# Fillers between the first-stage pieces taken out, a piece's folding moved to VectorE, and three pieces of work placed elsewhere in the start of a fused FFT and MLP kernel

## The chip, the cores and the metric

The kernel runs on one core of one Trainium2 chip. Its engines are TensorE (PE, matmuls into PSUM, with weight loads shown apart as PEld), VectorE (DVE), ScalarE (ACT), GpSimd (POOL) and SyncE (SP, which here only issues DMAs). The metric is device time in microseconds. The profile numbers time from the start of the profiled span.

## The reference

```python
x: (8, 3008, 256) float32         # 8 batches, 3008 = 47 * 64 rows, 256 columns
w_in: (256, 2048), w_out: (2048, 256)   # float64 as they arrive

X = fft(fft(x, axis=1), axis=2).real.astype(float32)
x = X.reshape(24064, 256)
h = x @ w_in
g = h * clip(h + 3, 0, 6) / 6
out = (g @ w_out).astype(float32)
```

A two-dimensional Fourier transform of each batch, of which the real part goes through an MLP with a hard-swish between its two products.

## The kernel before

**The transform.** The 3008 rows are taken as 47 x 64. Stage 1 is a transform of length 47 over the slow index, a matmul with the tables F; stage 2 joins the twiddles and the transform of length 64, a matmul with the tables T. The transform along the 256 columns is multiplied into `w_in` ahead of time by `fold_w_in` (C times a piece of `w_in` gives columns of W1, and one row of them goes by small DMAs into WN). Symmetry of a real input halves the work: rows n and 64 - n, and columns d and 256 - d, are added or subtracted first. That is the "fold". `fold_half(hb, m, part, eng)` does it for one piece of a single batch: part 0 adds the partner rows (fetched reversed in row order by a gather on GpSimd's DMA queue), part 1 adds and subtracts the mirrored columns into a new tile y. For batch 0, all pieces but one skip part 1's sums and differences: there TensorE does them, by reading the tile forward and backward and accumulating both in PSUM.

**The pieces.** The batches are worked in pairs. In the first pair, batch 0 and batch 1 are separate halves (`halves[0]`, `halves[1]`), each of four pieces in the order m = 3, 0, 1, 2 (`ORDER`). `stage1_early` takes one piece of batch 0: a few tiny matmuls into pt (column 128), then the piece's own into two PSUM banks (`ps1`, lines 320 to 330), then copies to an SBUF tile z (lines 336 to 338; the last of the last piece is VectorE's, the others ScalarE's), then DMAs of z to DRAM (zd). Only the rows that the first two groups need go at once (line 347); the rest is put into the list `later`, of which four transfers are issued at the end of step 1 and four at the end of step 3. A piece's PSUM banks come from a pool of four, its pt tiles from one of three. Tile z takes a buffer from a different pool for each piece: twice zpool, then ypool, then cpool.

**Groups.** `load_g_half` brings a group back from DRAM (line 414), `stage2_half` (line 433) makes q of it with a copy by ScalarE (line 436), `spread_half` and `spread_by_pe` copy its last row to all partitions (qn). Four groups per half feed eight chunks of 256 columns.

**The weights.** They arrive as float64, in 16 pieces of 128 x 512 numbers (`PIECES`; two of `w_in`, two of `w_out`, and again). Each piece j is loaded through GpSimd's DMA queue (`load_w`, lines 713 and 717) and turned to float32 in five parts: `exponent_a` (ScalarE, line 733, two activations into PM), `exponent_b` (TensorE, line 745, two matmuls into ex or spare), `exponent_c` (ScalarE, line 748), `mantissa` (VectorE, lines 756 and 757, into top), and `join` (VectorE, lines 765 or 771, into wi or G). `head_b(j)` is the mantissa and then, for j = 4 to 9, the load of piece j + 6. `mix_w_out` (GpSimd, lines 780 to 783) forms the combined blocks of G that later chunks need.

**Steps.** There are 384 steps, one for each chunk and each of eight parts of the hidden width. A step's MLP is `mlp1` (TensorE: products u and v, line 523, from a pool of three banks), `activate` (VectorE: s from u, WN and qn, line 532, then u and v, lines 542 and 544; ScalarE: t, line 569; VectorE: the gate, a, line 572), `combine` (GpSimd: c, line 586), and `mlp2` (TensorE, line 616, seven products for eight). Steps 0 to 7 are the first chunk, while the weights are still being prepared: there `mlp2_first` (line 596) uses eight plain products and needs no combine, and `first_steps` (even steps) and `second_steps` (odd) write out by hand how the weights' parts and the MLP's follow each other. Other work is put in at the start of a step by `beside` (`put(t, ...)`: step t): loads of T, groups, the folding and stage 1 of batch 1.

**What sets the order.** Nothing is reordered: each engine runs its instructions in the order in which the code issues them, and semaphores hold one until its data and its buffer are there. So a place in the code is a place in every queue that the call uses. `keep_awake(n)` (line 814) is n matmuls of 128 x 512 whose result nobody reads, called fillers here; the profile names them "awake" and shows two records for each. In the start they stand between the pieces (line 894), after them, and between the exponents' matmuls (lines 902 and 907). `see` (line 863) is a GpSimd copy that holds GpSimd's queue until the first group is back from DRAM; the loads of weight pieces 4 to 9 stand behind it.

Of the kernel before, what the change touches and what calls it, by code (L numbers as in the profile page):

```python
# [58 lines left out]
def kernel(  # L59
# [10 lines left out]
    nc = tc.nc  # L70
# [10 lines left out]
    XC = 4  # L81
    NS = N2 // 2
    NXC = NS // XC
    NM = NXC // 2
# [51 lines left out]


    ORDER = [NM - 1] + list(range(NM - 1))

    def x_tile(pool=xpool, tag="x"):  # L140
        return pool.tile([P, XC, D], F32, tag=tag, name="xt")
# [58 lines left out]
    def fold_half(hb, m, part, eng):  # L200
        xt, xr = hb.x[m][0:PX - 1], hb.xr[m][0:PX - 1]
        n = XC if m < NM - 1 else XC - 1
        a, r = xt[:, 0:n, :], xr[:, XC - 1:(XC - 1 - n) if n < XC else None:-1, :]
        lo, up = slice(0, N1), slice(PB, PB + N1)
        tt = eng.tensor_tensor
        if part == 0:
            sums = [(a, r)] + ([(xt[lo, n:XC, :], xr[lo, 0:1, :])] if n < XC else [])
            for a, r in sums:
                tt(a[:, :, 1:P], a[:, :, 1:P], r[:, :, D - 1:P:-1], op=AL.add)
                tt(a[:, :, D - 1:P:-1], a[:, :, D - 1:P:-1], r[:, :, 1:P], op=AL.add)  # L210
            return
        if hb.b == 0 and n == XC:
            tt(a[:, :, 0:P + 1:P], a[:, :, 0:P + 1:P], r[:, :, 0:P + 1:P], op=AL.add)
            return
        y = ypool.tile([PX - 1, XC + 1, D], F32, tag="y", name="y")
        hb.y[m] = y
        near, far = xt[:, :, 1:P], xt[:, :, D - 1:P:-1]
        tt(y[:, 0:XC, 1:P], near, far, op=AL.add)
        tt(y[:, 0:XC, P + 1:D], near, far, op=AL.subtract)
        tt(y[:, 0:n, 0:P + 1:P], a[:, :, 0:P + 1:P], r[:, :, 0:P + 1:P], op=AL.add)  # L220
        if n < XC:
            tt(y[lo, n, 0:P + 1:P], xt[lo, n, 0:P + 1:P], xr[lo, 0, 0:P + 1:P], op=AL.add)
            h = xr[up, 0, :]
            tt(y[up, XC, 1:P], h[:, 1:P], h[:, D - 1:P:-1], op=AL.add)
            tt(y[up, XC, P + 1:D], h[:, 1:P], h[:, D - 1:P:-1], op=AL.subtract)
            eng.tensor_copy(y[up, XC, 0:P + 1:P], h[:, 0:P + 1:P])
            eng.tensor_copy(y[up, n, 0:P + 1:P], xt[up, n, 0:P + 1:P])
        del hb.x[m], hb.xr[m]
# [74 lines left out]
    def stage1_early(hb, m):  # L303
        cosine, sine = slice(0, P + 1), slice(P + 1, D)
        last = m == NM - 1
        y = hb.y.pop(m) if last else hb.x[m]
        pt = [ps_h.tile([P, 2, 1], F32, tag="uv", name="pt") for h in range(2)]
        ps = [bank([P, 2, D], "ps1") for h in range(2)]
        quarters = [(i, h, 1 if last and h and i else 2) for i in range(2) for h in range(2)]
        for i, h, n in quarters:  # L310
            o = pt[h][i * PB:(i + 1) * PB]
            nc.tensor.matmul(o[:, 0:n], table(5, h), y[rows(h), 2 * i:2 * i + n, P:P + 1], start=True, stop=True,
                             skip_group_check=True)
            for k in range(2 if n < 2 else 0):
                nc.tensor.matmul(o[:, 1], table(k + 1, h), y[rows(h), XC - 1 + k, P:P + 1], start=(k == 0),
                                 stop=(k == 1), skip_group_check=True)
        if last:
            for i, h, n in quarters:
                o = ps[h][i * PB:(i + 1) * PB]
                nc.tensor.matmul(o[:, 0:n], table(0, h), y[rows(h), 2 * i:2 * i + n], start=True, stop=(n == 2),  # L320
                                 skip_group_check=True)
                for k, (j, cs) in enumerate([(XC - 1, cosine), (XC, cosine), (XC - 1, sine), (XC, sine)] if n < 2 else ()):
                    nc.tensor.matmul(o[:, 1, cs], table(k + 1, h), y[rows(h), j, cs], start=False, stop=(k % 2 == 1),
                                     skip_group_check=True)
        else:
            back = slice(D - 1, P, -1)
            for k, (t, to, fr) in enumerate([(0, cosine, cosine), (0, sine, slice(1, P)),
                                             (0, slice(1, P), back), (6, sine, back)]):
                for i, h, n in quarters:
                    nc.tensor.matmul(ps[h][i * PB:(i + 1) * PB, :, to], table(t, h), y[rows(h), 2 * i:2 * i + 2, fr],  # L330
                                     start=(k == 0), stop=(k > 1), skip_group_check=True)
        k = ORDER.index(m)
        pool, tag = ((zpool, "z"), (zpool, "z"), (ypool, "y"), (cpool, "c"))[k]
        z = pool.tile([PX, 2, 2, D + 1], F32, tag=tag, name="z")
        for h in range(2):
            nc.scalar.copy(z[:, h, :, D:], pt[h][0:PX])
        nc.scalar.copy(z[:, 0, :, 0:D], ps[0][0:PX])
        (nc.vector.tensor_copy if k == NM - 1 else nc.scalar.copy)(z[:, 1, :, 0:D], ps[1][0:PX])
        if not first.zd:
            first.zd[0] = dpool.tile([NG, 2 * KK, 2, NS, D + 1], F32, tag="zd0", name="zd")  # L340
        zd = first.zd[0][:].rearrange("g k c (h n) d -> (g k c) h (n d)", h=2)
        n0 = 2 * 4 * KK
        for i in range(2):
            n = (m * XC + 2 * i) * (D + 1)
            dst = zd[:, :, n:n + 2 * (D + 1)]
            src = z[i * PB:i * PB + PZ].rearrange("p h n d -> p h (n d)")
            (nc.scalar if k == NM - 1 and i else nc.sync).dma_start(out=dst[0:n0], in_=src[0:n0])
            later.append((dst[n0:], src[n0:]))
# [540 lines left out]
    for k, m in enumerate(ORDER):  # L889
        for part in range(2):  # L890
            fold_half(hb, m, part, nc.vector)
        stage1_early(hb, m)
        if k < NM - 1:
            keep_awake(1)
    load_g_half(hb, 0)

    seen = wpool.tile([P, 1], F32, tag="seen", name="seen")
    see(hb.g[0][:, 0, 0:1])
    for j in range(4, 10):
        load_w(j)  # L900

    keep_awake(2)
    for j in range(2, 4):
        exponent_a(j)
        mantissa(j)
        exponent_b(j)
        keep_awake(2)
    for j in range(2, 4):
        tail(j)

# [9 lines left out]
    def beside(p):  # L920
        ahead, behind = {}, {}

        def put(t, f, *a, at=ahead):
            at.setdefault(t, []).append((f, a))
# [3 lines left out]
        if p == 0:  # L928
            for gr in range(1, NG):
                put(gr + 1, load_t, gr)  # L930
            put(1, load_g_half, halves[0], 1)
            put(4, stage2_half, halves[0], 1)
            put(5, spread_half, halves[0], 1)
            put(NF - 1, close_w)
            for i, t in enumerate((3, 5, 7, 8)):
                put(t, mix_w_out, i)
            for gr in range(2, NSG):
                put(8 * gr - 10, load_g_half, halves[0], gr)
                put(8 * gr - 5, stage2_half, halves[0], gr)
                put(8 * gr - 4, spread_half, halves[0], gr)  # L940

            hb = halves[1]
            for k, m in enumerate(ORDER):
                put((1, 5, 8, 11)[k], take_half, hb, m, *((cpool, "c") if k == 0 else ()))
                put((1, 5, 8, 11)[k], load_half, hb, m, nc.sync)
                for part in range(2):
                    put((4, 6, 11, 14)[k] + part, fold_half, hb, m, part, nc.gpsimd)
                put((8, 10, 15, 18)[k], stage1_quarters, hb, m, at=behind)
            for gr in range(NSG):
                put(8 * gr + 23, load_g_half, hb, gr)  # L950
                put(8 * gr + 27 - (gr == 0), stage2_half, hb, gr)
                put(8 * gr + 28 - (gr == 0), spread_half, hb, gr)
# [75 lines left out]
    def second_steps(s):  # L1028
        j = 2 * s + 4
        if j - 2 < len(PIECES):  # L1030
            head_b(j)
            join(j)
            head_b(j + 1)
            if s == 1:
                mlp2_first(*chunk(s), halves=(0,))
                exponent_b(j + 1)
            exponent_c(j + 1)
            if j + 2 < len(PIECES):
                head(j + 2)
            join(j + 1)  # L1040
            if j + 3 < len(PIECES):
                head(j + 3)
            if s > 1:
                mlp2_first(*chunk(s), halves=(0,))
            mlp1(*chunk(s + 1))
            return
        mlp1(*chunk(s + 1))
        combine(*chunk(s + 1))
        mlp2_first(*chunk(s), halves=(0,))
        mlp1(*chunk(s + 2))  # L1050
        mlp2_first(*chunk(s), halves=(1,))
# [117 lines left out]
```

## Time and profile before

| | us |
|---|---|
| median of 3 runs (1943.94 to 1944.84) | 1944.27 |
| the profiled execution | 1943.62 |
| its span, from the first to the last instruction | 1941.9 |
| PE busy | 1924.4 (99%) |
| PE weight loads busy | 1659.3 (85%) |
| DVE busy | 1423.9 (73%) |
| ACT busy | 680.7 (35%) |
| POOL busy | 1435.6 (74%) |

In the lines below, a row of a timeline is: start, duration, engine, line, operation, output <- inputs, and in brackets how long the engine stood idle before it and what ended that. A row of the chain is: start, duration, what. "DMA share" is the mean busy share of the core's 16 DMA engines. A matmul in float32 shows as two records. Durations of matmuls hold the pipeline's end, so rows of one engine overlap a little. A wait for several semaphores is put down to the one that came last.

### The profile page before, as it was taken

What the parts mean: (1) busy time and instruction counts of PE and PEld (TensorE: products, weight loads), DVE (VectorE), ACT (ScalarE), POOL (GpSimd) and SP (SyncE); (2) the same over time, 40 slices, a digit from 0 to 9 for tenths busy, and PEclk for the clock granted to TensorE, in tenths of its full rate; (3) what the DMA queues carried; (4) which work ended last, traced back from release to release, by engine and by line L of the source; (5) the groups of instructions that cost most, each with busy time, mean ns of one, the idle gap of its engine ahead of it and who ended that gap; (6) DMA issues with size and microseconds to landing.
All of it is one profiled execution on the core that took longest, in us unless ns stands there. A gap on an engine that the chain in (4) does not pass through costs nothing.

```text
span 1941.9 us, 28190 instructions
## 1 busy us (share of the span) xinstructions
PE 1924.4 (99%) x9354; PEld 1659.3 (85%) x9354; DVE 1423.9 (73%) x2754; ACT 680.7 (35%) x1165; POOL 1435.6 (74%) x1644
## 2 busy tenths in 40 slices
PE   9999999999999999999999999999999999999998
PEld 5578888888988888888898888888899888888887
DVE  5876776677777777777787777777778777777777
ACT  5633333333333333333333333333333333333332
POOL 3397888887678877787678877878666667666665
PEclk9999999999999999999999999999999999999999
DMA  7532222311112222111111221222110101101000
GB/s 251 134 80 55 50 73 69 79 47 32 38 33 50 60 71 55 44 50 33 36 36 47 55 55 44 50 53 51 35 28 20 28 17 27 32 13 28 20 19 20
DMA packets 154520, 98.08 MB, mean 51 GB/s; under 512 B 121987, under 2 KB 136126, under 8 KB 154374
## 3 DMA queue, kind: packets, MB, share of 16 engines
q1 hardware_dynamic: 143106, 59.71, 12.8%
q0 software_dynamic: 10560, 36.35, 6.6%
q8 instruction: 73, 1.20, 0.3%
q14 instruction: 73, 0.60, 0.1%
q10 hardware_dynamic: 708, 0.23, 0.1%
HBM read 58.92 MB, written 37.32 MB: 50 GB/s over the span
## 4 chain that ended last, share of the span: by engine, by line
PE 93%; DVE 3%; ACT 1%; DMA 1%; POOL 1%; issue 1%; SPq 0%; DVEq 0%; ACTq 0%; POOLq 0%
PE acc L616 56%; PE v L523 16%; PE u L523 16%; PE ps L472 2%; PE ps L273 1%; DVE a L572 1%; DVE s L532 1%; PE awake L814 1%; ACT t L569 1%; DMA st<-in_moe_w_in_dram 0%; DVE o L677 0%; DVE u L553 0%; PE ps L433 0%; POOL c L586 0%; PE ps L330 0%
## 5 line engine op out<-in xcount | busy, mean ns | idle before, releaser
L586 POOL TENSOR_TENSOR c<-a 128x512 f32<-128x512 f32 (+1 forms) x375 | 468.1, 1248 | 355.5 <-PE acc L616 319.9
L616 PE MATMUL acc<-c,G 128*128 128x256 f32 (+1 forms) x3008 | 697.9, 375 | 0.9 <-POOL c L586 0.8
L569 ACT ACTIVATE t<-u,half 128x512 f32<-128x512 f32 (+1 forms) x384 | 260.6, 679 | 1145.4 <-DVE u L542 1066.0
L616 PEld LDWEIGHTS acc<-c,G 128*128 128x128 f32 x3008 | 566.6, 191 | 71.5 <-POOL c L586 2.1
L532 DVE SCALAR_TENSOR_TENSOR s<-qn,WN,u 128x256 f32<-128x256 f32 (+1 forms) x768 | 330.4, 472 | 345.5 <-PE u L523 340.0
L616 PE MATMUL acc<-a,G 128*128 128x256 f32 (+1 forms) x2256 | 542.1, 376 | 0.0
L616 PEld LDWEIGHTS acc<-a,G 128*128 128x128 f32 x2256 | 422.9, 190 | 71.9 <-issue 20.2
L523 PE MATMUL v<-q,W 127*128 127x256 f32 (+1 forms) x1536 | 389.6, 376 | 2.0 <-DVE a L572 2.0
L523 PE MATMUL u<-q,W 128*128 128x256 f32 (+1 forms) x1536 | 388.3, 376 | 0.2 <-ACT q L436 0.2
L572 DVE SCALAR_TENSOR_TENSOR a<-t,u 128x512 f32<-128x512 f32 (+2 forms) x448 | 264.0, 601 | 101.2 <-ACT t L569 97.6
L523 PEld LDWEIGHTS v<-q,W 127*128 127x128 f32 x1536 | 288.9, 190 | 42.0 <-DVE a L572 2.3
L523 PEld LDWEIGHTS u<-q,W 128*128 128x128 f32 x1536 | 286.6, 191 | 36.7 <-issue 2.4
L586 POOL TENSOR_TENSOR c<-c,a 128x256 f32<-128x256 f32 (+1 forms) x375 | 268.3, 715 | 29.4
L586 POOL TENSOR_TENSOR c<-a,c 128x256 f32<-128x256 f32 (+1 forms) x375 | 268.3, 715 | 29.4
L542 DVE TENSOR_TENSOR u<-s,v 128x512 f32<-128x512 f32 x352 | 245.1, 696 | 37.0 <-DVE s L532 0.5
L572 DVE SCALAR_TENSOR_TENSOR a<-t,v 128x512 f32<-128x512 f32 (+1 forms) x480 | 263.7, 566 | 0.1
L569 ACT ACTIVATE t<-v,half 128x512 f32<-128x512 f32 (+1 forms) x384 | 260.3, 678 | 0.2 <-PE acc L616 0.2
L544 DVE TENSOR_TENSOR v<-v,s 128x512 f32<-128x512 f32 x352 | 244.1, 693 | 0.0
L586 POOL TENSOR_TENSOR r<-w,e 128x256 f32<-128x256 f32 (+1 forms) x92 | 88.8, 986 | 3.6
L626 ACT ACTIVATE e<-acc 128x512 f32<-128x512 f32 (+2 forms) x184 | 83.3, 544 | 0.0
L677 DVE STREAM_TRANSPOSE o<-r 128x256 f32<-128x256 f32 (+1 forms) x192 | 72.5, 415 | 0.3
L586 POOL TENSOR_TENSOR w<-w,e 128x512 f32<-128x512 f32 (+1 forms) x46 | 57.5, 1249 | 3.6
(128 smaller groups left out, 776.6 us busy)
## 6 DMA issues: line engine op xcount, KB each, us to landing
out_dram<-o SPq DMA_DIRECT2D x747, 32.0 KB
g<-zd SPq DMA_DIRECT2D x42, 256.0 KB
zd<-z SPq DMA_DIRECT2D x48, 192.0 KB
xt<-in_x_dram POOLq DMA_DIRECT2D x22, 256.0 KB, 3.7
st<-in_moe_w_in_dram POOLq DMA_DIRECT2D x8, 512.0 KB, 6.4
st<-in_moe_w_out_dram POOLq DMA_DIRECT2D x8, 512.0 KB, 7.4
qn<-qd SPq DMA_DIRECT2D x16, 256.0 KB
xt<-in_x_dram POOLq DMA_DIRECT2D x17, 192.0 KB, 3.9
```

What stands on the lines that cost most here:

```text
L273: nc.tensor.matmul(ps[b][h * PB:(h + 1) * PB, 0:n], F[rows(b), 0:PB], y[rows(b), 2 * h:2 * h + n], start=True, stop=not last, skip_group_c ...
L472: nc.tensor.matmul(ps[:, blk, u * P:n].rearrange("p (b k) -> p b k", b=2), g[:, kk, blk * (P + 1):blk * (P + 1) + P], T[:, :, gr, blk, kk, ...
L523: nc.tensor.matmul(ps[:, i, 0:nq], W1[r, blk, f * P:(f + 1) * P], q[r, blk, of:of + nq], start=True, stop=True)
L532: nc.vector.scalar_tensor_tensor(s[:, i, 0:nq], qn[:, of:of + nq], WN[:, f:f + 1], u[:, i, 0:nq], op0=AL.mult, op1=AL.add)
L542: nc.vector.tensor_tensor(u[:], s[:], v[:], op=AL.add)
L544: nc.vector.tensor_tensor(v[:], v[:], s[:], op=AL.subtract)
L569: nc.scalar.activation(t, h, AF.Relu, bias=half[:], scale=scale)
L572: nc.vector.scalar_tensor_tensor(dst, t, 1.0, h, op0=AL.min, op1=AL.mult)
L586: (eng or nc.gpsimd).tensor_tensor(out, in0, in1, op=AL.add)
L616: nc.tensor.matmul(ch.acc[i // 2][:, i % 2, 0:ch.n], G[:, i, fc, :], mv, start=(fc == 0 and i % 2 == 0), stop=(fc == NF - 1), skip_group_c ...
L626: nc.scalar.mul(ch.e[:, k:i + 1, 0:ch.n], ch.acc[i // 2][:, 0:i + 1 - k, 0:ch.n], 1.0 / WS)
L677: nc.vector.transpose(o[:, 0:n // DH, h], ch.r[:, m, h, 0:n].rearrange("p (j i) -> p j i", i=DH))
```

## The change

- The three fillers between the first-stage pieces go, and one of the four after the weights' exponents that precede the second stage (`keep_awake(4 - j)`: two after piece 2, one after piece 3).
- The third piece of batch 0 (m = 1) is, like the first, folded wholly by VectorE, into a y tile; TensorE then does four matmuls of 512 columns for it. Its z comes from the activations' pool (apool) in place of ypool, and the list `later` is put in another order, so that this piece's remaining rows are written first.
- The second stage of batch 0's second group moves from the start of step 4 to step 3, ahead of the products of the next step.
- The first x of batch 1 is loaded through GpSimd's queue right behind weight pieces 4 to 9, in place of SyncE's queue at step 1.
- In step 1 the mantissa of piece 9, and with it the load of piece 15, comes after the MLP's first product and activation for step 2.

```diff
+    FULL = (ORDER[0], ORDER[2])
...
-        if hb.b == 0 and n == XC:
+        if hb.b == 0 and m not in FULL:
...
-        y = hb.y.pop(m) if last else hb.x[m]
+        y = hb.y.pop(m) if m in FULL else hb.x[m]
...
-        if last:
+        if m in FULL:
...
-        pool, tag = ((zpool, "z"), (zpool, "z"), (ypool, "y"), (cpool, "c"))[k]
+        pool, tag = ((zpool, "z"), (zpool, "z"), (apool, "a"), (cpool, "c"))[k]
...
         stage1_early(hb, m)
-        if k < NM - 1:
-            keep_awake(1)
+    later[:] = later[4:6] + later[0:4] + later[6:8]
     load_g_half(hb, 0)
...
     for j in range(4, 10):
         load_w(j)
+    take_half(halves[1], ORDER[0], cpool, "c")
+    load_half(halves[1], ORDER[0], nc.gpsimd)

     keep_awake(2)
     for j in range(2, 4):
         exponent_a(j)
         mantissa(j)
         exponent_b(j)
-        keep_awake(2)
+        keep_awake(4 - j)
...
             put(1, load_g_half, halves[0], 1)
-            put(4, stage2_half, halves[0], 1)
             put(5, spread_half, halves[0], 1)
...
             for k, m in enumerate(ORDER):
-                put((1, 5, 8, 11)[k], take_half, hb, m, *((cpool, "c") if k == 0 else ()))
-                put((1, 5, 8, 11)[k], load_half, hb, m, nc.sync)
+                if k > 0:
+                    put((5, 8, 11)[k - 1], take_half, hb, m)
+                    put((5, 8, 11)[k - 1], load_half, hb, m, nc.sync)
...
             if j + 3 < len(PIECES):
-                head(j + 3)
+                exponent_a(j + 3)
+                if s > 1:
+                    head_b(j + 3)
             if s > 1:
                 mlp2_first(*chunk(s), halves=(0,))
+            if s == 3:
+                stage2_half(halves[0], 1)
             mlp1(*chunk(s + 1))
+            if s == 1:
+                head_b(j + 3)
```

## The prediction

> **What bounds the kernel now.** I read the page's first part and its chain, then the busy time by stretch, then the chain in order of time over the first 120 us, and last each engine's timeline there. The stretches (columns: us; then PE, weight loads, VectorE, ScalarE, GpSimd busy with counts; granted clock; DMA share; GB/s):
>
> ```profile
> span 1941.9 us, 28190 instructions
> 0.00:36.00 36.00, 33.23 (x220) 17.48 (x220) 17.63 (x45) 20.78 (x34) 13.84 (x23) 1.00 0.70 218
> 36.00:60.00 24.00, 22.59 (x83) 14.21 (x82) 19.14 (x36) 16.33 (x28) 10.29 (x15) 1.00 0.80 256
> 60.00:80.00 20.00, 18.54 (x71) 11.95 (x70) 18.03 (x33) 13.42 (x22) 10.69 (x17) 1.00 0.57 159
> 105.00:120.00 15.00, 14.10 (x76) 10.39 (x75) 9.88 (x20) 4.73 (x9) 14.04 (x18) 1.00 0.28 70
> 120.00:400.00 280.00, 279.33 (x1343) 239.35 (x1342) 198.90 (x356) 99.71 (x173) 235.93 (x264) 1.00 0.27 65
> ```
>
> TensorE is busy nearly all the time, 279.33 of 280 us once the kernel is under way. Work that nothing touches follows the first 120 us, so whatever TensorE gains there reaches the end, unless a wait eats it. Within them it stands idle for 2.77, 1.41, 1.46 and, from 105, 0.90 us (each stretch less its busy time). But busy is not useful: the fillers ("awake") count as busy. The chain (start, us, what):
>
> ```profile
> 18.45 1.05 PE awake L814 x2
> ...
> 21.51 1.05 PE awake L814 x2
> ...
> 24.56 1.05 PE awake L814 x2
> ...
> 25.84 1.84 PE ps L330 x32
> 27.70 0.70 DVE z L338
> ...
> 33.21 1.72 PE awake L814 x4
> 34.93 0.91 PE ps L433 x8
> ```
>
> The four first-stage pieces run in a fixed rhythm, piece, filler, piece, filler, without a gap. After them come the weights' exponents with fillers, then the second stage at 34.93.
>
> **The change, part by part.**
>
> *Three fillers between pieces go.* 3 x 1.05 = 3.15 us of the chain, if the next piece is ready. VectorE's rows:
>
> ```profile
> 18.67 0.17 DVE L213 TENSOR_TENSOR xt<-xt 111x8 f32<-111x8 f32 x1
> 20.07 0.69 DVE L209 TENSOR_TENSOR xt<-xt 111x508 f32<-111x508 f32 x1 [1.23 <-DMA xt<-in_x_dram,IX]
> 21.27 0.17 DVE L213 TENSOR_TENSOR xt<-xt 111x8 f32<-111x8 f32 x1
> 22.04 0.59 ACT L338 COPY z<-ps 112x512 f32<-112x512 f32 x1
> ```
>
> The second piece can start at 18.45 and end near 20.5. The third fold was ready at 18.84, the fourth at 21.44, so folds do not hold it up.
>
> *Third piece folded fully.* TensorE gets 4 matmuls of 512 columns in place of 16 of 254 to 258. Nearest rows, both with the pipeline's end in them:
>
> ```profile
> 22.63 1.93 PE L330 MATMUL ps<-xt,F 47*64 47x258 f32 x32
> 105.61 1.08 PE L359 MATMUL ps<-y,F 47*64 47x512 f32 x8
> 14.56 0.68 DVE L219 TENSOR_TENSOR y<-xt 111x508 f32<-111x508 f32 x1
> ```
>
> -0.85 us on TensorE. VectorE gets two more 4 x 127 operations, some 0.6 us each from start to start: 1.2 us, which fit into the 1.23 us that it idled for the fourth piece's x. The fourth fold still ends near 21.45; without that pause it, and the fourth piece with it, would come up to 1.2 us later. The fourth piece waits for ScalarE to clear the second piece's banks: that piece ends near 20.5, two copies (0.59) and the small ones run to some 21.85, TensorE comes at 21.6. I charge 0.25. So the fourth piece ends 3.15 + 0.85 - 0.25 = 3.75 us sooner. If the fillers' time were wholly lost to waits, 0.85 would be left; without the 0.25 it is 4.0.
>
> *One filler less before the second stage* (2 of 4 records, half of 1.72): 0.86. Its cover is the group's arrival from DRAM, which GpSimd sees:
>
> ```profile
> 33.89 0.18 POOL L863 COPY seen<-g 128x1 f32<-128x1 f32 x1 [18.44 <-DMA g<-zd]
> 24.00:26.00 2.00, 2.00 (x30) 0.79 (x26) 0.00 (x0) 1.18 (x4) 0.00 (x0) 1.00 0.35 55
> ```
>
> 33.89 against 34.93: 1.04 us of slack. The write-out follows the fourth piece; the DMA share has fallen to 0.35 by 24 us, when it now starts, so I let the group come 3.75 sooner (30.14) and TensorE 3.75 + 0.86 = 4.6 (30.33). The next late thing is that group, 0.2 us behind. **Term A: 4.6, between 0.85 + 0.86 = 1.7 and 4.9.**
>
> *Mantissa of piece 9 behind step 2's activation.* The chain and timelines, in before's time:
>
> ```profile
> 56.70 0.49 DVE s L532
> 59.48 1.13 PE L523 MATMUL v<-q,W 127*128 127x256 f32 x4 [1.18 <-DVE a L572]
> 55.14 0.42 DVE L756 TENSOR_SCALAR top<-st 128x512 int32<-128x512 int32 x1
> 55.59 0.69 DVE L757 SCALAR_TENSOR_TENSOR top<-st,top 128x512 f32<-128x512 uint32 x1
> 64.89 1.07 DVE L756 TENSOR_SCALAR top<-st 128x512 int32<-128x512 int32 x1
> 65.99 1.23 DVE L757 SCALAR_TENSOR_TENSOR top<-st,top 128x512 f32<-128x512 uint32 x1
> 64.67 0.99 POOL L209 TENSOR_TENSOR xt<-xt 111x381 f32<-111x381 f32 x1 [3.95 <-DMA xt<-in_x_dram]
> ```
>
> VectorE's 1.06 us (55.14 to 56.20) come off ahead of step 2. But its second "s" is released by the WN transfer at 56.70, so the 1.18 us hole at 59.48 stays. **Term B: 0, at most 1.18**, if WN lands sooner. The 1.06 us come back between 60.1 and 61.2, ahead of step 3. There lies a trap: the same pair took 0.42 and 0.69 alone, 1.07 and 1.23 beside GpSimd's fold. If the moved pair met GpSimd, VectorE would be 1.2 us later still. Piece 15's load now waits for that mantissa, and behind the load on GpSimd's queue stand the mixing of the weights and the fold, so I expect no meeting there. GpSimd's 3.95 us of waiting for x, ahead of its fold at 64.67, hide this new wait of some 4.5 us all but 0.5: x is there long before, and the fold comes at about 65 as it did. The Trainium skill, "SBUF — State Buffer", section "Who interferes with whom", states that a VectorE operation with two SBUF inputs, or in a two-port mode, shares a port with GpSimd's reads; the two slow rows agree. By that rule, were the new x (already there) to let GpSimd fold just then, term C below would be near 0.
>
> *Second group's second stage ahead of step 4's products.*
>
> ```profile
> 72.31 0.88 DVE s L532 x2
> 74.72 0.69 DVE L572 SCALAR_TENSOR_TENSOR a<-t,u 128x512 f32<-128x512 f32 x1
> 68.97 2.76 ACT L733 ACTIVATE PM<-st,bias 128x512 uint8<-128x512 int16 x4
> 75.25 0.58 ACT L436 COPY q<-ps 128x512 f32<-128x512 f32 x1
> 75.88 0.59 PE L745 MATMUL ex<-PM,E 128*128 128x512 f16 x2 [1.46 <-ACT q L436]
> 77.77 0.86 PE v L523 x4
> ```
>
> The q copy stands on ScalarE behind step 4's relu; now it follows PM, ends by 72.3, and the 1.46 us hole at 75.88 goes. Next late is step 5's v: it takes the bank that step 4's gate (74.72, 0.69) frees, and VectorE is 1.06 late, so v starts at 76.5 instead of 77.77, and the products behind it (v takes 0.86) at 77.4 instead of 78.63. **Term C: 1.2, between 0 and 1.46.** The new u and v lie after the 0.9 us second stage, done by 72.5; VectorE wanted them at 72.31 and now near 73.4.
>
> *x of the second batch on GpSimd's queue.* Three issues (0.62 each, by SyncE's last of them) and the gather (1.00) come to 2.9 us and lie in GpSimd's 4.42 us of waiting:
>
> ```profile
> 43.12 0.72 POOL L717 DMA_DIRECT2D st<-in_moe_w_out_dram  x1 [4.42 <-DVE top L756]
> 45.21 1.00 POOL L172 DMA_INDIRECT xt<-in_x_dram,IX  x1 [0.30 <-issue]
> 56.24 0.62 SPq L197 DMA_DIRECT2D xt<-in_x_dram  x1
> ```
>
> Behind them on that queue stand the loads of pieces 10 and 11, the first to be late if 4.42 us do not do. Their bytes also queue behind 0.92 MB of x (twice 112 rows of 4 KB), 3.6 us at the 256 GB/s of 36 to 60. Both are covered by some 15 us, since the mantissa of piece 10 comes only at 64.89: 0. Without that cover it would cost TensorE those 3.6 us. SyncE loses three issues (the last at 56.24), so the group's second load and the leftover rows of z go out sooner; TensorE waits for neither now. The z of the third piece in the activations' pool: the leftovers written first are its own; 0. From 80 us on, VectorE, SyncE and GpSimd hang on TensorE's progress and move with it; the 0.90 us for GpSimd's products at 105 to 120 stays.
>
> **Sum.** 4.6 + 0 + 1.2 = 5.8 us. The profiled execution took 1943.62 us, 1.72 around its span; 1937.8. The median of the runs is 0.65 higher: 1938.5.
>
> **Rivals.** *Both holes close*: WN lands sooner and C is whole, A without its 0.25: 4.9 + 1.18 + 1.46 = 7.5, 1936.8. For it: SyncE and the DMA queues are freer. Against: WN's issues come before all that was removed.
>
> *Partly handed back*: the group from DRAM does not follow, or the moved mantissa meets GpSimd. With A = 3 and C = 0: 3.0, 1941.3. For it: only 0.2 us of slack left at 30.3. Against: the DMA share of 0.35 from 24 us.
>
> *The change does not bite*: the fillers only filled, and waits of the same length appear. A = 1.7, C = 0: 1942.6. Against: data for pieces 2, 3 and 4 are ready by the rows above.
>
> *Slower: the clock falls.* The fillers are named for keeping TensorE awake. At the kernel's end it idles from 1932.45, and the clock falls:
>
> ```profile
> 1930.99 1.46 PE L616 MATMUL acc<-c,G 128*128 128x192 f32 x8
> 1935.00:1942.00 7.00, 0.00 (x0) 0.00 (x0) 0.72 (x3) 0.00 (x0) 0.00 (x0) 0.66 0.25 55
> ```
>
> 0.66 over 7 us is 4.8 us at half: it fell some 4.8 us after the last matmul. If the quarter-array pieces, now on end from 16.6, did not count as work and the clock stood at half until the second stage, 13 us of work would double: 1944.27 - 5.8 + 13 = 1951.5. It loses from 5.8 us of work done at half rate, and shows as slower from 9.7. Against: the longest gap that I find in the new chain is some 0.5 us (the exponents' wait). The Trainium skill, "TensorE: Matmul & The Clock Gate", section "What's actually happening", puts the fall after an idle window of some 3.4 us; by that rule, as by the end's row, no gap here is long enough.
>
> **How the numbers follow.** Forecast (gain 4.6 to 6.6, 1937.6 to 1939.7) 0.52; both holes 0.16; partly handed back 0.18; does not bite 0.07; clock 0.07. About 0.2%, 3.9 us, is what a measurement of this kernel can tell. Faster: 0.52 + 0.16 + a third of the third, 0.74; same: the rest of it and the fourth, 0.19; slower 0.07. Range 1936.5 to 1942.3: both holes to most of the partly handed back, 0.84.
>
> **What would show it.** Right: pieces back to back from 18.4, the fourth ended near 24; the second stage near 30.3; no gap at the exponent after the q copy; the hole before v of step 3 still near 1.2, and a small one before v of step 5; clock 1.00. Wrong: a wait for g before the second stage over 0.5 us; VectorE's mantissa of piece 9 over 1.5 us; GpSimd's products waited for by more than 0.9 us at 100 to 115; a clock below 1.

## The result

The changed kernel takes 1940.45 us (median of 13 runs, 1938.39 to 1942.11) and the kernel before 1943.85 (13 runs beside them, 1942.70 to 1945.04): 3.4 us less, a ratio of 0.9981 with a 95% interval from 0.9972 to 0.9990. The direction and the range held; the size is some 60% of the 5.8 us forecast, and just short of the 0.2% that the text took as the bound of "faster". The profiled execution took 1940.75 us, 0.3 above the median. Its busy time by stretch (columns as in the prediction's first fence):

```profile
span 1939.0 us, 28126 instructions
0.00:36.00 36.00, 32.25 (x203) 18.65 (x204) 21.30 (x52) 22.01 (x37) 17.78 (x28) 1.00 0.76 247
36.00:60.00 24.00, 21.75 (x71) 12.73 (x70) 19.09 (x36) 16.48 (x27) 7.01 (x10) 0.94 0.95 279
60.00:80.00 20.00, 20.00 (x76) 12.74 (x75) 18.71 (x32) 13.66 (x23) 13.11 (x20) 0.99 0.30 79
```

From 60 to 80 the 1.46 us of idle time are gone, as forecast. From 36 to 60 there are 2.25 us of it where there were 1.41, the granted clock has fallen to 0.94, and the DMA share has risen from 0.80 to 0.95. That stretch was to stay as it was; here gain was given back. The chain of the start (start, us, what) carries no filler between pieces any more; the only fillers left in it stand among the weights' exponents:

```profile
20.04 0.29 PE pt L313 x8
...
21.56 1.83 PE ps L331 x32
...
23.42 0.70 DVE z L339
...
26.78 1.72 PE awake L815 x4
...
29.79 0.64 issue
30.43 1.14 PE ps L434 x8
```

The fourth piece's copy stands at 23.42 (27.70 before), the second stage at 30.43 (34.93 before). Both kernels do the same work up to their first piece, but the piece itself begins at another time in each execution:

```profile
16.57 0.29 PE L312 MATMUL pt<-y,F 47*64 47x2 f32 x8
```

in the timeline of before, and in that of after

```profile
15.91 0.29 PE L313 MATMUL pt<-y,F 47*64 47x2 f32 x8
20.04 0.29 PE L313 MATMUL pt<-y,F 47*64 47x2 f32 x8 [0.40 <-DVE y L221]
30.40 0.18 POOL L864 COPY seen<-g 128x1 f32<-128x1 f32 x1 [14.50 <-DMA g<-zd]
30.43 1.13 PE L434 MATMUL ps<-T,g 128*128 128x128 f32 x8 [0.64 <-issue]
56.29 1.49 PE L524 MATMUL v<-q,W 127*128 127x256 f32 x4 [2.25 <-DVE a L573]
72.76 0.59 PE L746 MATMUL ex<-PM,E 128*128 128x512 f16 x2
```

So 0.66 us of what the two traces seem to differ by is no work of the change. All comparisons below are counted from that first record; over all the kernels run here it lay between 15.65 and 17.53. Counted so:

| us after the first piece's first matmul | before | after | sooner by |
|---|---|---|---|
| copy of the fourth piece | 11.13 | 7.51 | 3.62 |
| first group seen back from DRAM | 17.32 | 14.49 | 2.83 |
| second stage begins | 18.20 | 14.52 | 3.68 |
| v of step 3 | 42.91 | 40.38 | 2.53 |
| second group's second stage | 55.08 | 52.51 | 2.57 |
| end of the span | 1925.33 | 1923.09 | 2.24 |

The second stage wins 3.68. The hole ahead of v of step 3 has grown from 1.18 to 2.25 us and takes 1.07 of it. The second group's second stage looks 2.57 sooner, but it now stands ahead of u and v (0.87 and 0.86), so 0.84 of gain is left at that place: 1.7 more went between. It went to the clock. Slices of two microseconds show it (the granted clock is the third number from the end):

```profile
54.00:56.00 2.00, 0.04 (x1) 0.00 (x0) 1.75 (x3) 1.17 (x2) 0.00 (x0) 1.00 1.00 332
56.00:58.00 2.00, 1.71 (x5) 1.39 (x6) 1.97 (x5) 2.00 (x5) 0.00 (x0) 0.73 1.02 399
58.00:60.00 2.00, 2.00 (x3) 0.68 (x2) 1.94 (x4) 0.47 (x1) 1.46 (x2) 0.50 0.50 134
60.00:62.00 2.00, 2.00 (x6) 0.92 (x5) 1.80 (x3) 1.23 (x2) 1.77 (x3) 0.91 0.78 250
```

The clock stood at half from 56.93 to 60.34 (finer slices give the ends; 0.73 and 0.91 above are the slices in which it fell and rose), 3.41 us, in which 1.7 us of work at full speed were done. That leaves 3.68 - 1.07 - 1.7 = 0.9. The span ends 2.24 sooner, so from there to the end 1.4 us come back, which is about the 1.46 us hole at the q copy.

What opened the hole stands on VectorE and in the chain of after. The second "s" of step 2 waits for the small WN transfer, and "a" and then v follow it:

```profile
48.32 5.17 DMA WN<-W
...
53.51 0.49 DVE s L533
...
55.55 0.70 DVE a L573
...
57.77 4.77 PE acc L597 x8
...
75.51 3.44 PE acc L597 x8
```

The transfer in the chain of before:

```profile
52.59 4.09 DMA WN<-W
```

From the copy of W that it carries, the transfer (0.5 KB) landed after 5.17 us in place of 4.09. (The eight acc matmuls behind v show the fallen clock once more: 4.77 us, where eight at 75.51 took 3.44.) What is different around the transfer is the DMA share. Before, in the 4 us around its issue:

```profile
50.00:52.00 2.00, 2.00 (x8) 1.29 (x7) 1.86 (x4) 2.00 (x5) 0.00 (x0) 1.00 0.12 31
52.00:54.00 2.00, 2.00 (x9) 1.32 (x8) 1.93 (x6) 1.39 (x4) 0.79 (x1) 1.00 0.29 33
```

and after, likewise:

```profile
46.00:48.00 2.00, 2.00 (x8) 1.15 (x7) 1.86 (x5) 2.00 (x5) 0.14 (x1) 1.00 1.03 220
48.00:50.00 2.00, 2.00 (x10) 1.43 (x8) 1.93 (x5) 1.39 (x3) 0.87 (x2) 1.00 1.02 293
```

The engines that were idle are full. That gives the theory to test (called Q below): the 0.92 MB of x, now between weight pieces 4 to 9 and pieces 10 and 11 on GpSimd's queue, still move when the WN transfer is issued, and it comes late behind them. Its rival (M): the moved mantissa changed VectorE's order, and the hole comes from there.

### The profile page after: what moved, and what is told of

Its sections match the earlier page's. It is cut to its first block, busy times and chain, and to the rows that moved or that the text cites. A ratio compares the mean times of both kernels' runs of the same rounds, so it can differ in the third digit from the quotient of the medians.

```text
span 1939.0 us, 28126 instructions
## 1 busy us (share of the span) xinstructions
PE 1920.7 (99%) x9322; PEld 1652.9 (85%) x9322; DVE 1426.0 (74%) x2756; ACT 681.5 (35%) x1165; POOL 1440.7 (74%) x1647
## 4 chain that ended last, share of the span: by engine, by line
PE 93%; DVE 2%; POOL 1%; DMA 1%; ACT 1%; issue 1%; SPq 0%; ACTq 0%; DVEq 0%; POOLq 0%
PE acc L617 56%; PE v L524 16%; PE u L524 16%; PE ps L473 2%; PE ps L274 1%; PE acc L597 1%; POOL c L587 1%; DVE a L573 1%; DVE s L533 0%; PE ps L434 0%; ACT t L570 0%; PE spare L798 0%; DVE o L678 0%; DMA st<-in_moe_w_in_dram 0%; DMA WN<-W 0%
```

## The experiments

The medians of before that stand beside a set of runs are 1943.76 (31 runs, e1 to e4), 1943.79 (25, e6 to e9) and 1943.68 (20, e5 and e10 to e12).

**x of the second batch back on SyncE (e1).** All of the change but that part:

```diff
-    take_half(halves[1], ORDER[0], cpool, "c")
-    load_half(halves[1], ORDER[0], nc.gpsimd)
...
-                if k > 0:
-                    put((5, 8, 11)[k - 1], take_half, hb, m)
-                    put((5, 8, 11)[k - 1], load_half, hb, m, nc.sync)
+                put((1, 5, 8, 11)[k], take_half, hb, m, *((cpool, "c") if k == 0 else ()))
+                put((1, 5, 8, 11)[k], load_half, hb, m, nc.sync)
```

> The changed kernel with the first x of batch 1 back on SyncE's queue at step 1, all else as changed. Theory Q (the early x fills the DMA queues when the small WN transfers of step 2 go, so step 2's second s is late, the hole ahead of step 3's v grows, and the clock falls behind it): the transfer from the W copy to the second s goes from 5.2 back to about 4.1 us or less, the hole from 2.25 to 1.2 or less, the clock stays 1.00, and the time is 1.5 to 2.5 us below the changed kernel, 1938 to 1939. Rival M (the moved mantissa, or the lack of fillers, makes the hole): the hole stays above 2 us, the clock still falls, the time stays within 0.7 us of the changed kernel.

1938.78 us (9 runs, 1937.97 to 1939.68; ratio 0.9976, 0.9966 to 0.9986), 1.7 below the changed kernel. Its windows and its timeline:

```profile
36.00:60.00 24.00, 23.18 (x79) 13.40 (x78) 20.17 (x39) 17.17 (x28) 6.83 (x9) 1.00 0.87 265
48.00:50.00 2.00, 2.00 (x8) 1.15 (x7) 1.88 (x5) 1.40 (x3) 0.79 (x1) 1.00 0.07 19
55.53 1.13 PE L524 MATMUL v<-q,W 127*128 127x256 f32 x4 [0.82 <-DVE a L573]
```

The engines have a free stretch again at 48 (share 0.07), the hole is 0.82, the clock 1.00. All nine runs lie below the changed kernel's median, though the two intervals of the ratio overlap. Of the parts of the change, the early x is one that costs time.

**That part alone in the kernel before (e2).** The reverse of the diff above, in before.

> The kernel before with one part of the change alone: the first x of batch 1 on GpSimd's queue behind weight pieces 4 to 9. Theory Q: the hole ahead of step 3's v grows from 1.18 to about 2.2 us, and the time is 1 us above the kernel before, up to 2.7 where the clock falls behind it. Rival M: the hole stays 1.2, the clock 1.00, the time within 0.5 us of before.

1943.96 us (11 runs; ratio 1.0002, 0.9993 to 1.0011). No difference.

```profile
60.23 1.13 PE L523 MATMUL v<-q,W 127*128 127x256 f32 x4 [1.30 <-DVE a L572]
```

The hole is 1.30 (1.18 before): the early x alone is harmless. So Q as first put is incomplete. The x must meet something that another part of the change brings.

**The mantissa of piece 9 put back (e4).**

```diff
-                exponent_a(j + 3)
-                if s > 1:
-                    head_b(j + 3)
+                head(j + 3)
...
-            if s == 1:
-                head_b(j + 3)
```

> The changed kernel with the mantissa of piece 9 back in its old place. Theory Q: step 2's second s still waits for WN, so the hole stays 2 us or more and the time within 0.7 us of the changed kernel; VectorE is 1.06 us earlier at step 4, which nothing waits for. Rival M: the hole falls to 1.2 or below and the time by 1 to 2.5 us.

1941.45 us (11 runs, 1938.11 to 1943.38; ratio 0.9986, 0.9977 to 0.9995).

```profile
58.45 2.08 PE L524 MATMUL v<-q,W 127*128 127x256 f32 x4 [3.43 <-DVE a L573]
```

With the old order on VectorE the hole does not shrink, it grows to 3.43, and the clock falls. M is refuted. The same edit on top of e1 (e8) asks what the move is worth when the hole is small:

> As e1, and the mantissa of piece 9 back in its old place, so that the move of the mantissa is priced without the early x. The prediction gave it nothing at step 3 (term B = 0, WN is last) and charged it a quarter of a us at step 5's v: the time equals e1 within 0.4 us, the hole stays at 0.8 to 1.2. If the move is what shortens the hole: hole 1.2 or more, time 0.4 to 1 us above e1.

1938.47 us (8 runs; ratio 0.9973, 0.9962 to 0.9983), 0.3 from e1 and with a hole of 1.09. The move is worth nothing that can be measured, as the prediction's term B = 0 had it.

**The three fillers and the fourth back (e6),** everything else as changed:

```diff
+        if k < NM - 1:
+            keep_awake(1)
...
-        keep_awake(4 - j)
+        keep_awake(2)
```

> The changed kernel with the four fillers back (three between pieces, one ahead of the second stage). It loses their 4.0 us but for what the fold and group waits had kept (0.4 and 0.6). Theory Q in full (the collision needs both the early x and the start's gain, which brings WN's issue closer to the loads): the hole falls to 1.4 or less, the clock stays 1.00, and the time is about 1941.5, 1 us above the changed kernel. If the collision needs only the early x: hole over 2, clock falls, 1943 or more. If the missing fillers themselves made the clock fall: clock 1.00 with a hole over 2.

1942.30 us (10 runs; ratio 0.9994, 0.9984 to 1.0003), 0.8 more than I expected.

```profile
58.93 1.13 PE L524 MATMUL v<-q,W 127*128 127x256 f32 x4 [1.17 <-DVE a L573]
```

x is early here, and the hole is 1.17 and the clock 1.00. With e1 and e2 this gives the condition: the long hole needs both the early x and the sooner start. The reading that fits, argued and not tested by itself, is this. The weight loads start when the first group is seen back; before, that is 0.88 us ahead of the second stage (17.32 and 18.20 in the table), after, it is 0.03 ahead. TensorE, and with it the copy of W and the issue of WN, has come 0.85 us nearer to the loads. With x between the loads there is no room for that. The chains and slices of these runs fit it: the transfer is slow where the engines are still full while it is under way. In e2 the slices from 46 to 52 are full as well (1.01 to 1.07), but the transfer starts at 53.20, in a slice with a share of 0.87, and takes 4.23 us. In after and e4 it starts at 48.32 and 49.30, the share is 1.01 to 1.03 from 48 to 52, and it takes 5.17 and 6.35.

**The hole ahead of step 3 filled (e3).** Two fillers stand ahead of the products of step 3, so that the clock does not fall (the call for that step passes `fill=2`):

```diff
-    def mlp1_products(ch, fc, between=None):
+    def mlp1_products(ch, fc, between=None, fill=0):
...
+            for i in range(fill if not blk else 0):
+                nc.tensor.matmul(ps[:].rearrange("p i n -> p (i n)"), ones[:], C[:].rearrange("p h d -> p (h d)"),
+                                 start=True, stop=True)
```

> The changed kernel with two fillers (128 x 512, 1.72 us in all) in the hole, written into the bank of step 3's u ahead of its products. If the fall of the clock is a cost of its own, laid on top of the wait: the clock stays 1.00 from 36 to 66 us, the wait ahead of v shrinks to 0.5 as it is filled, and the time falls by 1 to 1.7 us, less what the fall does not take in every execution. If the fall costs nothing that waits do not hide: no change within 0.5 us.

1940.06 us (11 runs, 1939.30 to 1941.24; ratio 0.9982, 0.9973 to 0.9991).

```profile
36.00:60.00 24.00, 23.22 (x79) 13.56 (x78) 19.02 (x36) 16.64 (x28) 6.76 (x10) 1.00 0.92 280
56.70 1.13 PE L527 MATMUL v<-q,W 127*128 127x256 f32 x4 [0.78 <-DVE a L576]
67.14 1.05 PE L434 MATMUL ps<-T,g 128*128 128x128 f32 x8
```

The fillers' 1.72 us and 0.78 of idle time make 2.50, no shorter than the hole was, but the clock stays at 1.00. From v of step 3 to the second group's second stage this execution takes 10.44 us (67.14 - 56.70), the one of after 12.13 (68.42 - 56.29): 1.69 less, the price of the fall as counted above. The medians are only 0.4 apart, and the runs lie closer together (1.9 us from first to last in place of 3.7). That fits if only a part of after's executions lose the clock, and the mean granted clock that is noted for every run says so: every profile with a fall has 0.997 or 0.998 (0.998 alone does not tell, e7's profile has it without a fall), while seven of after's 13 runs have 0.999. Their median is 1939.68, that of the other six 1940.92. One of the seven took 1941.82, so the clock does not explain the whole spread.

**The third piece as it was (e7).**

```diff
-    FULL = (ORDER[0], ORDER[2])
+    FULL = (ORDER[0],)
```

> The changed kernel with the third piece's column sums back on TensorE. The prediction's -0.85 us on TensorE; but the trace showed a 0.40 us wait for the full fold and 0.64 us of waiting for the group ahead of the second stage. If the write-out and the group's load set the second stage: the second stage starts 0 to 0.4 us later, the time within 0.6 us of the changed kernel. If TensorE sets it: 0.85 us later.

1939.62 us (10 runs, 1938.29 to 1942.00; ratio 0.9981, 0.9972 to 0.9990): the ratio is that of the changed kernel.

```profile
54.90 1.13 PE L524 MATMUL v<-q,W 127*128 127x256 f32 x4 [1.25 <-DVE a L573]
```

The fourth piece's copy comes at 7.50 after the first piece's start. In after it was 7.51, and in the other executions with the full fold and without fillers 7.03 to 7.71. The full fold of the third piece, costed at 0.85 us of TensorE's time, was worth at most 0.5 in these executions and in after nothing: TensorE waited 0.40 for it (the row at 20.04).

e7 also has the early x and the sooner start (second stage at 14.39, after's 14.52), and yet its profile shows a hole of 1.25 and a full clock. So the two conditions are needed, but they don't bring the long hole in every execution. The third piece's order is not a third condition, as far as the noted clocks tell: two of e7's ten runs (1941.00 and 1941.78) have a mean clock of 0.997. So low it is nowhere in the runs of before, e1, e2, e3, e6, e8, e9 and e10; in e4, e5 and e11, which have both conditions, eight runs are at 0.997 or below, and the profile of one of these shows the fall.

**The second group's second stage back at step 4 (e5).**

```diff
+            put(4, stage2_half, halves[0], 1)
...
-            if s == 3:
-                stage2_half(halves[0], 1)
```

> The changed kernel with the second group's second stage back at the start of step 4. The prediction's term C: the wait of the exponents for the q copy returns (1.46 us before), and the time rises by 1.2 us over the changed kernel (0 to 1.5). If the early hole and the slower stretch before it had already covered that wait: under 0.4 us.

1942.88 us (10 runs, 1941.29 to 1944.01; ratio 0.9995, 0.9985 to 1.0004), 2.4 above the changed kernel, where 1.2 were expected.

```profile
57.63 1.73 PE L524 MATMUL v<-q,W 127*128 127x256 f32 x4 [2.22 <-DVE a L573]
74.92 0.59 PE L746 MATMUL ex<-PM,E 128*128 128x512 f16 x2 [0.66 <-ACT q L437]
```

The wait for the q copy is back at the exponent. By the ends of the spans, counted from the first piece, e5's execution is 1.24 behind after's, but 0.38 of that were there already at v of step 3 (57.63 - 16.87 = 40.76, after 40.38). The medians say 2.4; none of e5's ten runs has a mean clock of 0.999, so its median may hold the fall more often. That this part is a gain is shown; its size is open, between some 0.9 and 2.4.

**The weight loads held behind WN (e9).** If the WN transfer comes late because bulk loads are ahead of it, loads that wait for it should close the hole. On top of e1, GpSimd looks at WN before it issues the next three loads (`see`, as for the first group):

```diff
             if s == 1:
+                see(WN[:, NF + 2:NF + 3])
```

> As e1 (x back on SyncE's queue), and GpSimd, ahead of the load of piece 12, first reads the WN column that step 2's second s needs, so that the loads of pieces 12 to 15 start only when it has landed. Theory Q (bulk loads in flight are what makes WN late): WN lands about 2 us after its issue, step 2's second s waits no more, the hole ahead of step 3's v falls from 0.82 to 0.3 or less, and the time is 0.4 to 0.8 us below e1. If WN is late for its own sake (small transfers, order of issue on SyncE): the hole stays 0.8 and the time equals e1 within 0.4 us.

1937.24 us (6 runs, 1936.71 to 1938.91; ratio 0.9968, 0.9956 to 0.9980), 1.5 below e1, where 0.4 to 0.8 were expected. Counted from the first piece, the span of the profiled execution ends 0.7 before e1's (1935.4 - 16.90 and 1936.5 - 17.30); the intervals of the two ratios overlap, so the size of the gain is less sure than the closed hole:

```profile
50.64 0.18 POOL L864 COPY seen<-WN 128x1 f32<-128x1 f32 x1 [8.51 <-DMA WN<-W]
51.05 0.87 DVE L533 SCALAR_TENSOR_TENSOR s<-qn,WN,u 128x256 f32<-128x256 f32 x2
36.00:60.00 24.00, 24.00 (x84) 14.28 (x83) 20.83 (x39) 17.99 (x31) 8.12 (x12) 1.00 0.79 253
```

The two "s" run as a pair with no wait between, and TensorE is busy for the whole 24.00 us. What the prediction called the hole that stays (1.18) can be closed, and the WN transfer is what it hung on. The same line on top of the changed kernel, x still early (e11):

> The changed kernel, x early as changed, with the loads of pieces 12 to 15 held behind WN as in e9. If the bytes of x ahead of pieces 10 and 11 are what WN meets: the second s still waits for WN and the hole stays over 0.8, the time 0.7 us or more above e9. If only the loads of pieces 12 and 13 matter: the hole closes as in e9, and the time is that of e9 within 0.5 us.

1939.02 us (9 runs; ratio 0.9975, 0.9965 to 0.9985), 1.8 above e9.

```profile
53.30 0.87 DVE L533 SCALAR_TENSOR_TENSOR s<-qn,WN,u 128x256 f32<-128x256 f32 x2 [1.98 <-DMA WN<-W]
56.46 1.13 PE L524 MATMUL v<-q,W 127*128 127x256 f32 x4 [2.06 <-DVE a L573]
```

The chain of e11 and a window of it:

```profile
46.39 6.81 DMA WN<-W
48.00:50.00 2.00, 2.00 (x9) 1.22 (x8) 1.93 (x6) 1.38 (x4) 0.00 (x0) 1.00 1.01 307
```

GpSimd issues no load between 42.24 (piece 11) and 54.07, and still the engines are full at 48 to 50 and WN takes 6.81 us. This is the first of the step's two WN transfers; in after it took some 6.2 (its copy of W ended at 46.00, and the "s" that waited for it began at 52.22). What it meets are transfers issued before it: the weight pieces up to 11, pushed back by x. With e1 this is the place of the cost.

**The second x a step sooner (e10).** On top of e9, SyncE's issue of the next x at step 4 in place of 5, against the wait for GpSimd's products at 105 to 120 that the prediction let stand:

```diff
-                put((1, 5, 8, 11)[k], take_half, hb, m, *((cpool, "c") if k == 0 else ()))
-                put((1, 5, 8, 11)[k], load_half, hb, m, nc.sync)
+                put((1, 4, 8, 11)[k], take_half, hb, m, *((cpool, "c") if k == 0 else ()))
+                put((1, 4, 8, 11)[k], load_half, hb, m, nc.sync)
```

> As e9, and batch 1's second x is loaded at step 4 in place of step 5, ahead of step 4's WN transfers on SyncE's queue. TensorE's wait for GpSimd's products near 108 us (1.04 us in e9, 0.85 before) comes at the end of a chain that starts with this x landing at 95 to 98 us. If that chain sets it: GpSimd folds 10 us sooner, the wait falls under 0.3 us, the time is 0.5 to 1 us below e9, 1936.5. If GpSimd's own amount of work sets it: the same as e9 within 0.3 us.

1936.89 us (5 runs, 1936.34 to 1937.49; ratio 0.9963, 0.9949 to 0.9977): the best version here, 6.8 below the kernel before. The stretch from 105 to 120 of e9:

```profile
105.00:120.00 15.00, 13.90 (x70) 10.75 (x69) 9.99 (x20) 4.72 (x9) 14.11 (x16) 1.00 0.40 93
```

and of e10:

```profile
105.00:120.00 15.00, 15.00 (x77) 12.34 (x77) 10.31 (x20) 4.93 (x9) 13.43 (x15) 1.00 0.42 118
```

1.1 us of idle time are gone from it. The median gives back only 0.35 of that (the two sets of runs have their own before, 0.1 apart), less than these runs can tell from nothing. Nor do the spans show it whole, for e10's second stage happened to begin 1.22 us later after the first piece than e9's (14.93 and 13.71). From the second stage to the end e10 is 1.4 shorter (1935.2 - 31.82 and 1935.4 - 30.61).

**The changed kernel once more (e12),** for a second profile of it.

> The changed kernel itself, profiled once more. Its times spread over 3.7 us. If the clock falls in only some executions, with the length of the hole: this one shows either a hole of 2 us or more with the clock at half for one window behind it, near 1941 or above, or a shorter hole with the clock at 1.00 and 1939 or below.

One run, 1942.37 us.

```profile
57.25 1.53 PE L524 MATMUL v<-q,W 127*128 127x256 f32 x4 [2.69 <-DVE a L573]
```

The hole is 2.69, and the clock stood at half from 57.85 to 61.26: the first profile was no accident.

## Why the prediction was right, and where not

The time came into the range, but partly by luck: the slow end of the range was drawn for a late group and a meeting of the mantissa with GpSimd, and what took the gain was something else. Three of the prediction's own signs of being wrong showed: a wait of 0.64 us for the group (over 0.5), one of 1.07 for GpSimd's products (over 0.9), and a clock below 1.

- **Fillers between the pieces: right.** The fourth piece's copy comes 3.62 us sooner (3.75 forecast). But its parts were shared out wrongly: the third piece's fold was to give 0.85, and e7 shows between nothing and 0.5. VectorE was late for it by 0.40 in after; the pause for the fourth piece's x hid the added work from the fourth fold, not from the third.
- **Group from DRAM 0.2 behind: off by size.** It came 2.83 sooner, not 3.75, and TensorE waited 0.64. SyncE's queue from 14 to 30 shows a likely cause (engine and line, what ended the wait: us in total, times, longest), a write of z that waited 2.0 us (0.3 in before) for a transfer with which it has no data in common, WN:

```profile
SPq L348 <- DMA WN<-W: 2.2, 2, 2.0
```

  Term A is 3.7 in this execution, inside 1.7 to 4.9 and below 4.6. In e3 the same start gave 4.6 (second stage 13.64 after the first piece, 18.20 before), in e5 3.3 (14.93): it varies by execution. That the second stage's 30.43 lies so near the forecast 30.3 is luck, for after's first piece began 0.66 sooner.
- **Term B, 0 and at most a gain of 1.18: this step failed.** That the second "s" hangs on WN was read rightly, and the moved mantissa did nothing (e8). But the term was bounded on the gain side only. In the profiled execution it measured -1.07 for the hole and some -1.7 for the clock; executions that keep the clock lose less.
- **Early x at 0, "both are covered by some 15 us": this is the cause.** The text asked who stands behind x on GpSimd's own queue, and those loads are indeed not missed. It did not ask who else uses the 16 DMA engines in that stretch. The window of before with a share of 0.12 was the room in which SyncE's smallest transfer went through, and x filled it. e1 and e11 show the cost, e2 and e6 that a filled window costs little (holes of 1.30 and 1.17) as long as the start does not come sooner as well, e7 that it does not come out in every execution.
- **Term C, 1.2: right.** 1.4 are left for it in the count above (0.9 to 2.4 by e5); the q copy's wait is gone from the exponent (no idle time in the row at 72.76), and no hole ahead of v of step 5 shows in after. In e1 and e3, which have no long hole, the small one that was forecast is there (0.21).
- **The trap on VectorE: right.** The moved pair ran at its short durations, so it did not meet GpSimd:

```profile
56.81 0.42 DVE L757 TENSOR_SCALAR top<-st 128x512 int32<-128x512 int32 x1
57.27 0.69 DVE L758 SCALAR_TENSOR_TENSOR top<-st,top 128x512 f32<-128x512 uint32 x1
```

- **The clock: right for the pieces, wrong for the place.** It stayed at 1.00 over the quarter-array pieces on end. The statement that the longest gap of the new chain is some 0.5 us was wrong, since it followed from B = 0: a gap of 2.25 us opened at 54.04.
- **The wait for GpSimd's products at 105 to 120: right that it stays.** It is a little longer (1.07 in after's row):

```profile
111.35 2.32 PE L617 MATMUL acc<-c,G 128*128 128x256 f32 x8 [1.07 <-POOL c L587]
```

- **The sum.** Of the rivals, "partly handed back" comes nearest by its time (1941.3), not by its mechanism: neither the group nor the mantissa was the main cause. e1, the change without its x part, is 1938.78: the forecast's 1938.5 is what the rest of the change is worth.

## What to carry over

Ask of every bulk transfer that is moved not only what is queued behind it, but which small transfer of any other queue is issued in the stretch where the engines will now be full; look for the windows of low DMA share and for who uses them. A part that is harmless alone (e2) and one that only gains (the sooner start) can cost together, because the gain moves the waiting instruction nearer to the data. And price a wait that may grow by the clock too: here the fall cost more than the hole's growth.

## What the runs showed of the hardware

The granted clock fell after a shorter idle time than I had reckoned with. Holes of 0.78 to 1.30 us ahead of v of step 3 (before, e1, e2, e3, e6, e7, e8) left it at 1.00 up to 66 us, and so did the hole of 1.46 at the q copy in before up to 80. With holes of 2.06, 2.22, 2.25, 2.69 and 3.43 (e11, e5, after, e12, e4) it fell each time, between 0.1 us before work began again (e4) and 1.4 us after (e11), and in each it stood at half for 3.4 us. The Trainium skill, "TensorE: Matmul & The Clock Gate", section "What's actually happening", puts the fall after an idle window of some 3.4 us. The length of the fall agrees with that window (56.93 to 60.34 is 3.41); the idle time needed does not, since 2.06 us were enough. In the 3.41 us just ahead of after's fall TensorE was busy for 1.16:

```profile
53.52:56.93 3.41, 1.16 (x6) 0.70 (x5) 3.15 (x6) 2.10 (x4) 0.00 (x0) 1.00 0.97 341
```

So a stretch of that length need not be wholly idle; that the chip counts just this stretch is not shown.

Full DMA engines do not always move the same: at a share of 1.03 the stretch from 46 to 48 of after moved 220 GB/s, while in before

```profile
42.00:43.00 1.00, 1.00 (x5) 0.75 (x4) 0.97 (x3) 1.00 (x3) 0.00 (x0) 1.00 1.03 418
```

at the same share moved 418. In after and in e11, both with the early x, the rate stood at 200 to 230 GB/s from 42 to 48; in e1 it was 330 to 363 from 42 to 46. What halves the rate there, x's rows, its gather or something else, stays open; whether the early x would cost anything at the full rate is not shown.
